# Longformer attention into a gated GeGLU block: the order of the work between the first and the second chunk

## Chip, cores and metric

The kernel runs on one core of one Trainium2 chip. The metric is device time in microseconds (us) of one execution; the time before is the median of three runs.

## What is computed

The reference, cut to what matters:

```python
# q, k, v: 8 batches x 8 heads x 576 positions x 64; 8 global positions
scores = q @ k.T / 8
mask = (abs(i - j) <= 32) | is_global[i] | is_global[j]
attn = softmax(where(mask, scores, -1e9))
x = (attn @ v) as 4608 tokens x 512
g, val = x @ w_gate, x @ w_val            # 512 -> 1536
ffn = (gelu(g) * val) @ w_out             # 1536 -> 512
out = x + sigmoid(x @ w_res) * ffn
```

## The kernel before, in words

A batch has nine windows of 64 positions. The 72 windows are cut into nine chunks of eight, so that a chunk is 512 tokens: chunk 0 is windows 0 to 7 of batch 0, chunk 1 the last window of batch 0 and seven of batch 1. The loop over chunks (L806) runs the feed-forward block of chunk c and, among it, the attention of chunk c + 1. The engines follow the order of the code (the schedule is written by hand); each engine has its own queue, in order.

For one chunk the steps are, by name:
- **Gate and value halves** (`ffn_steps`, L621): for each of twelve column blocks j, four matmuls of 512 columns give `g_ps` and four give `v_ps`; ScalarE takes the Gelu of `g_ps` into `gsb` (L635) and VectorE multiplies `gsb` with `v_ps` into `ht` (L638, "the product").
- **Turns** (`turn_pair`, L445, batches 0 and 1 only): TensorE transposes a pair of heads of k and q (p = 0 to 3, and -1 for the last 64 positions) into a bank of PSUM; VectorE copies k into `kt`, ScalarE copies q into `qt`.
- **Scores** (`scores`, L543): 16 small matmuls for each of four head groups give two banks `sc`; ScalarE takes the Exp (for chunk 1 in place, in PSUM), VectorE multiplies with the mask into `pt` (L556). A call has two banks, and a quad is half a chunk.
- **Global rows and columns**: `global_scores` (L467, tile `sg`), `global_exp` (L484: three Exps of ScalarE, then `gt` times `maskr` on VectorE, L494), `global_rows` (L496: matmuls into `sn`, then the multiplication into `vgs` on VectorE, L513).
- **Values** (`local_values`, L562, and `values`, L578) for each of four tiles t of 128 tokens: 16 matmuls of `pt` with V and two or four with `gt` and `vgs` into `nd`; VectorE takes the reciprocal and writes `xtok`. `split` (L559) says whether `nd` is one two-bank tile of the pool `psn` (tag "nd") or two single banks.
- **turn_x** (L602): `xtok` transposed into `xt`, the next chunk's input.
- **Residual gate** (`gate`, `open_gate`, L652 to L663): four matmuls into `r_ps`, Tanh on ScalarE.
- **Thirds** (`third`, L680): `f_ps` summed over twelve j in three groups of four matmuls; after the last, VectorE (L689) and GpSimd (L691) make the output, and SyncE stores it.

PSUM has three pools: `psm` with four banks (tag "mm": `g_ps`, `v_ps`, half of the scores, `r_ps`, `f_ps`), `pss` with two (tag "sc": turns, the other scores, `turn_x`), and `psn` with one tile of two banks (tag "nd": `sg`, `sn`, `nd`, one after the other). A tile waits until the one that held its place before it has been read.

For chunk 0 the order between its feed-forward block and chunk 1 is written out by hand (L814 to L934). Blocks j = 2 to 9 run one after the other, with `turn(0)` and `turn(1)` inside blocks 8 and 9. Blocks 10 and 11 run as gate, Gelu, `turn(2)`, gate, Gelu, `turn(3)`, then a dummy Exp that loads ScalarE's table, value, product, `turn(-1)`, value, product. Then L892 to L933: scores of quad 0, `global_scores`, residual gates 0 and 1 ahead of the scores of quad 1, `global_rows`, gate 2, `values(1, 0)`, gate 3, and the thirds with the other values among them.

Weights and the inputs of batch 1 are loaded as float32 into spare places by SyncE's queue and cast by GpSimd. `load_piece(n)` and `cast_piece(n)` move the weights: pieces 0 to 11 gate and value weights, 12 and 13 the residual weights `wr_t`, 14 to 19 the output weights `wo_t`. `load_raw` and `cast_pair` move k and q of a pair; `load_vraw(1)` and `cast_v(1, c)` the V of batch 1 in five parts, and `shift_on_chip(n)` copies V shifted by 64 rows into `vo`. SyncE's order before: pieces 10 and 11, raw pairs 0, 1, 2, 3, -1, pieces 12 and 13, V, pieces 14 to 19. GpSimd's order before (L852 to L868): pairs 0, 1, 2, 3, -1, pieces 12 and 13, V, `shift_on_chip(0)`, pieces 14 to 19, `shift_on_chip(3)`.

Of the kernel before, what the change touches and what calls it, by code (L numbers as in the profile page):

```python
# [9 lines left out]
BF16 = mybir.dt.bfloat16  # L10
# [13 lines left out]
def kernel(  # L24
# [116 lines left out]
    def load_piece(n):  # L141
        nc.sync.dma_start(staged(n), pieces[n][0])

    def cast_piece(n, copy):
        copy(pieces[n][1], staged(n))
# [411 lines left out]
        return mask  # L557

    def split(c, t):  # L559
        return c == 0 and t % 2 == 0 or c > 1 and t % 2 == 1  # L560

    def local_values(c, t):  # L562
        if split(c, t):
            pool, tag = (pss, "sc") if c else (psm, "mm")
            nds = [pool.tile([128, 512], F32, name=f"nd{hf}", tag=tag) for hf in range(2)]
            nd = None
        else:
            nd = psn.tile([128, 2, 512], F32, name="nd", tag="nd")
            nds = [nd[:, 0, :], nd[:, 1, :]]
        wins = [divmod(CH * c + 2 * t + e, NW) for e in range(2)]  # L570
        for h in range(H):
            for e, (b, i) in enumerate(wins):
                vw = ve[b % 2][:, i // 2, h, :] if i % 2 == 0 else vo[b % 2][:, i // 2, h, :]
                nc.tensor.matmul(nds[h // 4][64 * e:64 * e + 64, VG * (h % 4):VG * (h % 4) + VG],  # L574
                                 pt[:, h, 2 * t + e, :], vw, start=(h % 4 == 0), stop=False)
        return nd, nds, wins

    def values(c, t, begun=None):  # L578
# [10 lines left out]
        if split(c, t):  # L589
            for hf in range(2):  # L590
# [8 lines left out]
        nc.vector.tensor_tensor(xtok[c % 2][:, t, :].rearrange("p (a h d) -> p a h d", a=2, d=D),  # L599
                                num[:, :, :, 0:D], view(rden, 0, 128, 0, [[4, 2], [1, 4], [0, D]]), ALU.mult)  # L600

    def turn_x(c, t):  # L602
        mine = xt[c % 2][:, :, 128 * t:128 * t + 128]
        if c > 1:
            nc.sync.dma_start(mine, xtok[c % 2][:, t, :], transpose=True)
            return
        tx = pss.tile([128, NKT, 128], BF16, name="tx", tag="sc")
        for kk in range(NKT):
            nc.tensor.transpose(tx[:, kk, :], xtok[c % 2][:, t, 128 * kk:128 * kk + 128], ident)  # L609
        (nc.vector.tensor_copy if c or t == 3 else nc.scalar.copy)(mine, tx)  # L610
# [10 lines left out]
    def ffn_steps(c, j):  # L621
        x, held = xt[c % 2], {}

        def product(what, w):
            def emit(c0, c1):
                if what not in held:
                    held[what] = psm.tile([128, 512], F32, name=f"{what}_ps", tag="mm")
                for kk in range(NKT):
                    nc.tensor.matmul(held[what][:, c0:c1], w[:, kk, 128 * j:128 * j + 128], x[:, kk, c0:c1],  # L629
                                     start=(kk == 0), stop=(kk == NKT - 1))  # L630
            return emit

        def gelu():
            held["s"] = work.tile([128, 512], BF16, name="gsb", tag="gsb", bufs=3)
            nc.scalar.activation(held["s"], held["g"], ACTF.Gelu, bias=0.0, scale=1.0)  # L635

        def mul():
            nc.vector.scalar_tensor_tensor(ht[:, j, :], held["s"], 0.5, held["v"], ALU.mult, ALU.mult)  # L638

        def end():  # L640
            gelu()
            mul()

        return {"g": product("g", wg_t), "v": product("v", wv_t), "gelu": gelu, "mul": mul, "end": end}
# [118 lines left out]
    for n in range(4):  # L763
# [4 lines left out]
            load_raw(1, "kq"[n - 2], 0, nc.sync)  # L768
        if n == 1:
            fill(band, 1.0, [([[-1, 64]], 1, 0, ALU.is_ge, 0.0), ([[1, 64]], -1, 64, ALU.is_ge, 0.0)])  # L770
    for p in (1, 2, 3, -1):
        for what in "kq":
            load_raw(1, what, p, nc.sync)
    for n in range(4, 12):
        cast_piece(n, POOL)
    for n in (12, 13):
        load_piece(n)
    values(0, 0, begun_v[0])
# [22 lines left out]
    def turn(p):  # L801
        for what in "kq":
            turn_pair(1, p, what)

    turns = {8: lambda: turn(0), 9: lambda: turn(1)}
    for c in range(NCH):  # L806
        b = c + 1
        if b < B and c:
# [3 lines left out]
                gather(what, (c + 1) // 2 if c % 2 else c // 2 + 1)  # L812
        held = None
        for j in range(NFF):  # L814
            if c == 0 and j == 10:
                last = [ffn_steps(0, n) for n in (10, 11)]
                last[0]["g"](0, 512)
                last[0]["gelu"]()
                turn(2)
                last[1]["g"](0, 512)  # L820
                last[1]["gelu"]()
                turn(3)

                nc.scalar.activation(none, none, ACTF.Exp, bias=0.0, scale=1.0)
                last[0]["v"](0, 512)
                last[0]["mul"]()
                turn(-1)
                last[1]["v"](0, 512)
                last[1]["mul"]()
            elif c or 1 < j < 10:  # L830
                ffn_in(c, j, turns.get(j) if c == 0 else None)
            if c == 0:
                if j == 0:
                    mask_rows(0, NW)
                elif j == 1:
                    mask_rows(NW, NWM)
                    zero_k(1)
                elif j == 2:
                    zero_gt(1, nc.vector)
                    zero_globals(1)  # L840
                    for n in range(1, B // 2):
                        nc.vector.tensor_single_scalar(idx[:, n:n + 1], idx[:, 0:1], float(2 * H * S * n), ALU.add)
                elif j == 3:
                    zero_v(1, nc.vector)
                elif j == 4:
                    double_qk(0, 1)
                elif j == 6:
                    got = turn_globals(0, 1)
                    for what in "kq":
                        DVE(compact[what][:, 0:1, :], got[what])  # L850
                    spread_qk(1, compact, 0, {"k": DVE, "q": ACT})
                elif j == 5:  # L852
                    for p in (0, 1, 2, 3, -1):
                        for what in "kq":
                            cast_pair(1, p, what, POOL)
                    load_vraw(1)
                    for n in (14, 15):
                        load_piece(n)
                    for n in (12, 13):
                        cast_piece(n, POOL)  # L860
                    for n in range(16, 20):
                        load_piece(n)
                    for c5 in range(5):
                        cast_v(1, c5, POOL)
                    shift_on_chip(0, POOL)
                    for n in range(14, 20):
                        cast_piece(n, POOL)
                    shift_on_chip(3, POOL)  # L868
# [19 lines left out]
        if c == 0:  # L888
            def third(t, n):
                work_f[4 * t + 1 + n]()  # L890

            scores(1, 0, (0,))(0, 2)  # L892
            got = global_scores(1)
            scores(1, 0, (1,))(0, 2)
            global_exp(1, *got)
            for t in range(2):
                gates[t][0](now=False)
            first = scores(1, 1, (0,))
            gates[0][1]()
            second = scores(1, 1, (1,))  # L900
            gates[1][1]()
            global_rows(1)
            first(0, 2)
            gates[2][0]()
            values(1, 0)
            gates[3][0]()
            second(0, 2)
            for n in (1, 2):
                shift_on_chip(n, ACT)
            for what in "kq":  # L910
                load_second(what)
            cast_second("k", 0, NQT, ACT)
            values(1, 1)
            third(0, 0)
            third(1, 0)
            third(2, 0)
            turn_x(1, 0)
            third(3, 0)
            values(1, 2)
            turn_x(1, 1)  # L920
            third(0, 1)
            cast_second("q", 0, 1, POOL)
            values(1, 3)
            third(1, 1)
            turn_x(1, 2)
            third(2, 1)
            third(3, 1)
            turn_x(1, 3)
            for t in range(4):
                third(t, 2)  # L930
                if t == 1:
                    turn_qk(2, "k")
            cast_second("q", 1, NQT, POOL)  # L933
            continue  # L934
        jobs = {n: [] for n in range(16)}
        if c + 1 < NCH:
# [8 lines left out]
            jobs[1] += [lambda: half(0), gates[-1][1], lambda: held_mask[0](0, 4)]  # L945
            jobs[3].append(lambda: half(1))

            def two(t0):
                both = [local_values(c + 1, t) for t in (t0, t0 + 1)]
                for t in (t0, t0 + 1):  # L950
                    values(c + 1, t, both[t - t0])
                for t in (t0, t0 + 1):
                    turn_x(c + 1, t)

            jobs[4].append(lambda: two(0))
            jobs[8].append(lambda: two(2))
            jobs[5].append(lambda: held_mask[1](0, 2))
            jobs[6].append(lambda: held_mask[1](2, 4))
        for n in range(16):
# [35 lines left out]
```

## Time and profile before

| | |
|---|---|
| median of three runs | 387.99 us (387.68 to 388.45) |
| the profiled execution's own time | 387.56 us |
| its span in the trace | 385.9 us |
| TensorE busy | 372.7 us, 97% of the span |
| VectorE, ScalarE, GpSimd busy | 52%, 44%, 44% |
| chain that ended last | TensorE 94%, VectorE 3%, ScalarE 2% |

The profile is of one execution. A busy TensorE is the sum of its matmuls, each with its way through the array at the end; matmuls overlap, so the distance from one start to the next is shorter than the duration shown. The chain that ended last goes back from the last instruction, at each step to what released it. Where TensorE is nearly always busy, only its waits and its own work set the time.

### The profile page before, as it was taken

To read this page: it belongs to the slowest core of one execution; us is meant where nothing else is said; L and a number is where in the kernel's file an instruction comes from. 1 tells how busy PE (TensorE), PEld (TensorE's weight loads), DVE (VectorE), ACT (ScalarE), POOL (GpSimd) and SP (SyncE) were. 2 spreads that over 40 slices of the span, in tenths; PEclk is the share of its full clock that TensorE was granted. 3 is DMA by queue.
4 is the path that set the end of the run, shared out by engine and by line. 5 is a ranking of instruction groups with operands and counts; after the bars stand their busy time and mean duration, and the time that the engine had idled before them with its cause. 6 is when DMAs were issued, how large, how long until landed. Compare 5 with 4: busy or idle time off the path is not lost.

```text
span 385.9 us, 8474 instructions
## 1 busy us (share of the span) xinstructions
PE 372.7 (97%) x3332; PEld 187.7 (49%) x3332; DVE 200.8 (52%) x467; ACT 169.8 (44%) x285; POOL 168.2 (44%) x203
## 2 busy tenths in 40 slices
PE   3989989999999999999999999999999999999996
PEld 2664555444544454445444544454445544544444
DVE  7767774446734573367334744564445534553422
ACT  4753684436333643355334633372337233723321
POOL 7688684868355524661466138712501210121012
PEclk9999999999999999999999999999999999999999
DMA  8999999799949923999299939994990410041002
GB/s 242 239 373 366 249 321 220 172 178 162 136 97 152 195 58 109 127 199 103 82 146 175 114 97 135 182 102 117 110 158 4 109 57 0 3 109 56 0 29 82
DMA packets 156810, 53.70 MB, mean 139 GB/s; under 512 B 140194, under 2 KB 147234, under 8 KB 156770
## 3 DMA queue, kind: packets, MB, share of 16 engines
q1 hardware_dynamic: 80832, 42.80, 46.2%
q0 software_dynamic: 75392, 9.84, 43.7%
q8 instruction: 26, 0.43, 0.5%
q10 hardware_dynamic: 546, 0.52, 0.4%
q14 instruction: 14, 0.11, 0.1%
HBM read 39.19 MB, written 9.44 MB: 126 GB/s over the span
## 4 chain that ended last, share of the span: by engine, by line
PE 94%; DVE 3%; ACT 2%; issue 1%; POOL 0%; DVEq 0%; POOLq 0%; ACTq 0%
PE g_ps L629 24%; PE f_ps L685 24%; PE v_ps L629 24%; PE r_ps L655 8%; PE nd L574 3%; PE nd L586 3%; PE sc L533 3%; PE ss L480 1%; PE sg L471 1%; PE sn L509 1%; PE tk L450 1%; PE tq L450 1%; PE tx L609 0%; PE sc L522 0%; PE f_ps L671 0%
## 5 line engine op out<-in xcount | busy, mean ns | idle before, releaser
L638 DVE SCALAR_TENSOR_TENSOR ht<-gsb,v_ps 128x512 bf16<-128x512 bf16 x108 | 74.1, 687 | 95.8 <-PE v_ps L629 91.3
L635 ACT ACTIVATE gsb<-g_ps 128x512 bf16<-128x512 f32 x108 | 64.4, 597 | 121.1 <-PE g_ps L629 118.8
L691 POOL TENSOR_TENSOR ob<-prb,xtok 128x512 f32<-128x512 f32 x35 | 40.2, 1152 | 166.5 <-DVE prb L689 166.5
L629 PE MATMUL g_ps<-xt,wg_t 128*128 128x512 bf16 (+1 forms) x456 | 111.9, 368 | 0.0
L629 PE MATMUL v_ps<-xt,wv_t 128*128 128x512 bf16 (+1 forms) x456 | 111.9, 368 | 0.0
L685 PE MATMUL f_ps<-wo_t,ht 128*128 128x512 bf16 x420 | 98.0, 379 | 0.0
L629 PEld LDWEIGHTS <-wv_t 128*128 128x128 bf16 x456 | 43.5, 98 | 49.1
L629 PEld LDWEIGHTS <-wg_t 128*128 128x128 bf16 x456 | 43.4, 98 | 48.7
L685 PEld LDWEIGHTS <-ht 128*128 128x128 bf16 x420 | 39.8, 98 | 45.6
L663 ACT ACTIVATE rsb<-r_ps 128x512 bf16<-128x512 f32 x36 | 21.7, 606 | 68.0 <-PE r_ps L655 68.0
L689 DVE SCALAR_TENSOR_TENSOR prb<-rsb,f_ps 128x512 f32<-128x512 bf16 x35 | 24.1, 688 | 52.3 <-PE f_ps L685 50.7
L655 PE MATMUL r_ps<-wr_t,xt 128*128 128x512 bf16 x144 | 36.7, 378 | 1.0 <-ACT rsb L663 1.0
L540 ACT ACTIVATE pt<-sc 128x512 bf16<-128x512 f32 x64 | 33.2, 607 | 4.0 <-PE sc L533 3.2
L91 POOL DMA_DIRECT2D q_st<-in_q_dram x25 | 21.4, 861 | 18.8 <-DMA qt<-q_st 17.9
L99 POOL DMA_DIRECT2D ve<-in_v_dram x30 | 25.5, 865 | 0.0
L556 DVE TENSOR_TENSOR pt<-pt,maskw 128x512 bf16<-128x512 bf16 x56 | 21.8, 421 | 4.1 <-ACT pt L540 2.8
L91 POOL DMA_DIRECT2D k_st<-in_k_dram x25 | 21.1, 876 | 4.4 <-DMA kt<-k_st 3.2
L655 PEld LDWEIGHTS <-xt 128*128 128x128 bf16 x144 | 13.5, 97 | 13.2 <-issue 0.9
L574 PEld LDWEIGHTS <-pt 128*64 128x64 bf16 x576 | 11.1, 110 | 9.3 <-issue 4.6
L599 DVE TENSOR_TENSOR xtok<-nd,rden 128x512 bf16<-128x512 f32 x20 | 13.8, 691 | 0.8
L593 DVE TENSOR_TENSOR xtok<-nd,rden 128x256 bf16<-128x256 f32 x32 | 13.6, 425 | 1.1
L574 PE MATMUL nd<-ve,pt 128*64 128x65 bf16 x320 | 13.5, 196 | 0.7 <-DVE xtok L599 0.6
(174 smaller groups left out, 294.1 us busy)
## 6 DMA issues: line engine op xcount, KB each, us to landing
out_dram<-ob SPq DMA_DIRECT2D x35, 256.0 KB, 2.2
vo<-ve SPq DMA_DIRECT2D x12, 260.0 KB, 5.5
q_st<-in_q_dram POOLq DMA_DIRECT2D x20, 128.0 KB, 6.0
k_st<-in_k_dram POOLq DMA_DIRECT2D x20, 128.0 KB, 6.7
ve<-in_v_dram POOLq DMA_DIRECT2D x18, 128.0 KB, 6.4
wo_t<-in_k_dram SPq DMA_DIRECT2D x8, 256.0 KB, 5.6
vraw<-in_q_dram SPq DMA_DIRECT2D x8, 256.0 KB, 6.8
extra<-in_moe_w_out_dram SPq DMA_DIRECT2D x4, 512.0 KB, 7.5
```

Of the source, the lines that this page charges most:

```text
L91: nc.gpsimd.dma_start(dst[0:n, r, :].rearrange("p (h d) -> p h d", d=D), src[b].rearrange("h s d -> s h d")[128 * r:128 * r + n])
L99: nc.gpsimd.dma_start(t[p0:p1, c, :, 0:D], v[b].rearrange("h s d -> s h d")[s0 + p0:s0 + p1])
L540: nc.scalar.activation(sc if stay else mine, sc, ACTF.Exp, bias=0.0, scale=SCALE)
L556: nc.vector.tensor_tensor(m, x, view(maskw, 0, 128, 64 * i0, [[0, 2], [64, 4], [1, 64]]), ALU.mult)
L574: nc.tensor.matmul(nds[h // 4][64 * e:64 * e + 64, VG * (h % 4):VG * (h % 4) + VG], pt[:, h, 2 * t + e, :], vw, start=(h % 4 == 0), stop=F ...
L629: nc.tensor.matmul(held[what][:, c0:c1], w[:, kk, 128 * j:128 * j + 128], x[:, kk, c0:c1], start=(kk == 0), stop=(kk == NKT - 1))
L635: nc.scalar.activation(held["s"], held["g"], ACTF.Gelu, bias=0.0, scale=1.0)
L638: nc.vector.scalar_tensor_tensor(ht[:, j, :], held["s"], 0.5, held["v"], ALU.mult, ALU.mult)
L655: nc.tensor.matmul(r_ps, xt[c % 2][:, kk, 128 * t:128 * t + 128], wr_t[:, kk, :], start=(kk == 0), stop=(kk == NKT - 1))
L685: nc.tensor.matmul(held["f"], ht[:, j, 128 * t:128 * t + 128], wo_t[:, j, :], start=(j == 0), stop=(j == NFF - 1))
L689: nc.vector.scalar_tensor_tensor(prb, held["r"], 1.0, held["f"], ALU.add, ALU.mult)
L691: nc.gpsimd.tensor_tensor(ob, prb, xtok[c % 2][:, t, :], ALU.add)
```

## The change

It reorders work between chunk 0 and chunk 1. The gate halves of blocks 8 to 11 run first, each followed by its Gelu and one turn (pairs 0, 1, -1, 2); then the value half of block 8, `turn(3)` and the dummy Exp. The value halves and products of blocks 9, 10 and 11 go between the scores of chunk 1. `global_exp` goes ahead of the scores of quad 0's second half, and the masks of quad 1's first half ahead of `global_rows`. All four residual gates go behind the values of tiles 0 and 1, which run as a pair (`two`). Tiles 1 and 3 of chunk 1 use split banks: tile 1 from `psm`, tile 3 from `pss`. `gsb` has five buffers in place of three. The loads: pair -1 comes ahead of pairs 2 and 3, V of batch 1 ahead of pieces 12 and 13 on SyncE's queue; on GpSimd the casts of 12 and 13 come behind those of V and `shift_on_chip(0)`; the loads of 18 and 19 come behind the casts of 12 and 13 in the code.

```diff
     def split(c, t):
-        return c == 0 and t % 2 == 0 or c > 1 and t % 2 == 1
+        return t % 2 == (1 if c else 0)
...
-            pool, tag = (pss, "sc") if c else (psm, "mm")
+            pool, tag = (pss, "sc") if c > 1 or c == 1 and t > 1 else (psm, "mm")
...
+    def two(c, t0):
+        both = [local_values(c, t) for t in (t0, t0 + 1)]
+        for t in (t0, t0 + 1):
+            values(c, t, both[t - t0])
...
-            held["s"] = work.tile([128, 512], BF16, name="gsb", tag="gsb", bufs=3)
+            held["s"] = work.tile([128, 512], BF16, name="gsb", tag="gsb", bufs=5)
...
-    for p in (1, 2, 3, -1):
+    for p in (1, -1, 2, 3):
         for what in "kq":
             load_raw(1, what, p, nc.sync)
     for n in range(4, 12):
         cast_piece(n, POOL)
+    load_vraw(1)
     for n in (12, 13):
         load_piece(n)
...
-            if c == 0 and j == 10:
-                last = [ffn_steps(0, n) for n in (10, 11)]
-                last[0]["g"](0, 512)
-                last[0]["gelu"]()
-                turn(2)
-                last[1]["g"](0, 512)
-                last[1]["gelu"]()
+            if c == 0 and j == 8:
+                late = [ffn_steps(0, n) for n in range(8, NFF)]
+                for steps, p in zip(late, (0, 1, -1, 2)):
+                    steps["g"](0, 512)
+                    steps["gelu"]()
+                    turn(p)
+                late[0]["v"](0, 512)
+                late[0]["mul"]()
                 turn(3)
-
                 nc.scalar.activation(none, none, ACTF.Exp, bias=0.0, scale=1.0)
-                last[0]["v"](0, 512)
-                last[0]["mul"]()
-                turn(-1)
-                last[1]["v"](0, 512)
-                last[1]["mul"]()
-            elif c or 1 < j < 10:
-                ffn_in(c, j, turns.get(j) if c == 0 else None)
+            elif c or 1 < j < 8:
+                ffn_in(c, j)
...
-                    for p in (0, 1, 2, 3, -1):
+                    for p in (0, 1, -1, 2, 3):
                         for what in "kq":
                             cast_pair(1, p, what, POOL)
-                    load_vraw(1)
-                    for n in (14, 15):
-                        load_piece(n)
-                    for n in (12, 13):
-                        cast_piece(n, POOL)
-                    for n in range(16, 20):
+                    for n in range(14, 18):
                         load_piece(n)
                     for c5 in range(5):
                         cast_v(1, c5, POOL)
                     shift_on_chip(0, POOL)
+                    for n in (12, 13):
+                        cast_piece(n, POOL)
+                    for n in (18, 19):
+                        load_piece(n)
                     for n in range(14, 20):
                         cast_piece(n, POOL)
...
+            late_value(1)
             scores(1, 0, (0,))(0, 2)
+            late_value(2)
             got = global_scores(1)
+            global_exp(1, *got)
             scores(1, 0, (1,))(0, 2)
-            global_exp(1, *got)
-            for t in range(2):
-                gates[t][0](now=False)
+            late_value(3)
             first = scores(1, 1, (0,))
-            gates[0][1]()
             second = scores(1, 1, (1,))
-            gates[1][1]()
+            first(0, 2)
             global_rows(1)
-            first(0, 2)
-            gates[2][0]()
-            values(1, 0)
-            gates[3][0]()
             second(0, 2)
+            two(1, 0)
+            for n in range(4):
+                gates[n][0]()
             for n in (1, 2):
                 shift_on_chip(n, ACT)
             for what in "kq":
                 load_second(what)
             cast_second("k", 0, NQT, ACT)
-            values(1, 1)
             third(0, 0)
             third(1, 0)
+            turn_x(1, 0)
             third(2, 0)
-            turn_x(1, 0)
+            turn_x(1, 1)
             third(3, 0)
-            values(1, 2)
-            turn_x(1, 1)
+            two(1, 2)
             third(0, 1)
             cast_second("q", 0, 1, POOL)
-            values(1, 3)
             third(1, 1)
```

(`late_value(n)` is the value half of `late[n]` and its product. The later chunks' own `two` is renamed, with the same work.)

## Rows read from the trace of the kernel before

**Rows 1.** Windows: stretch, us, busy us by engine, granted clock, DMA, GB/s
```profile
52.00:58.00 6.00, 4.76 (x89) 2.73 (x82) 4.69 (x10) 5.00 (x10) 4.75 (x6) 1.00 1.02 368
...
70.40:110.30 39.90, 39.90 (x351) 19.30 (x350) 21.41 (x48) 17.12 (x28) 25.01 (x29) 1.00 1.16 153
```

**Rows 2.** PE timeline from block 8's gate: start, us, instruction [idle before]
```profile
38.15 1.03 PE L629 MATMUL g_ps<-xt,wg_t 128*128 128x512 bf16 x4
39.01 0.39 PE L450 MATMUL tk<-ident,k_st 128*128 128x128 bf16 x4
39.23 0.39 PE L450 MATMUL tq<-ident,q_st 128*128 128x128 bf16 x4
...
48.47 0.43 PE L471 MATMUL sg<-qt,kgz 128*32 128x288 bf16 x8
...
49.42 0.41 PE L533 MATMUL sc<-qt,kt 64*128 64x64 bf16 x16
49.76 1.90 PE L655 MATMUL r_ps<-wr_t,xt 128*128 128x512 bf16 x8
...
52.23 0.46 PE L509 MATMUL sn<-ve,ptg 128*16 128x130 bf16 x20
53.66 1.02 PE L655 MATMUL r_ps<-wr_t,xt 128*128 128x512 bf16 x4 [0.97 <-ACT rsb L663]
```

**Rows 3.** PE timeline, first value matmuls to chunk 1's first gate half
```profile
54.61 0.45 PE L574 MATMUL nd<-ve,pt 128*64 128x65 bf16 x16
54.99 0.62 PE L586 MATMUL nd<-vgs,gt 128*128 128x260 bf16 x4
55.45 1.02 PE L655 MATMUL r_ps<-wr_t,xt 128*128 128x512 bf16 x4
...
70.19 1.03 PE L629 MATMUL g_ps<-xt,wg_t 128*128 128x512 bf16 x4
```

**Rows 4.** ACT (ScalarE) timeline, from pair 3's q copy to the global Exps
```profile
45.36 0.58 ACT L457 COPY qt<-tq 128x512 bf16<-128x512 bf16 x1
45.96 1.28 ACT L824 ACT_TABLE_LOAD   x1
...
47.37 0.73 ACT L455 COPY qt<-tq 64x256 bf16<-64x256 bf16 x2
48.56 1.07 ACT L540 ACTIVATE sc<-sc 128x512 f32<-128x512 f32 x2 [0.47 <-PE sc L533]
...
50.95 0.50 ACT L490 ACTIVATE ptg<-sg 128x192 bf16<-128x192 f32 x2
51.34 0.66 ACT L493 ACTIVATE gt<-sg 128x576 bf16<-128x576 f32 x1
```

**Rows 5.** DVE (VectorE) timeline, from block 10's product to vgs
```profile
46.25 0.69 DVE L638 SCALAR_TENSOR_TENSOR ht<-gsb,v_ps 128x512 bf16<-128x512 bf16 x1 [0.47 <-PE v_ps L629]
46.85 0.85 DVE L455 COPY kt<-tk 64x256 bf16<-64x256 bf16 x2
...
49.17 2.58 DVE L556 TENSOR_TENSOR pt<-sc,maskw 128x512 bf16<-128x512 f32 x4 [0.75 <-ACT sc L540]
52.03 0.57 DVE L494 TENSOR_TENSOR gt<-gt,maskr 128x576 bf16<-128x576 bf16 x1 [0.27 <-ACT gt L493]
52.74 0.70 DVE L513 TENSOR_TENSOR vgs<-sn,head 128x520 bf16<-128x520 f32 x1
```

**Rows 6.** POOL (GpSimd) timeline: last raw pair, residual piece 13, V's last part
```profile
43.59 0.61 POOL L267 CAST q_st<-vraw 128x512 bf16<-128x512 f32 x1
...
46.81 1.04 POOL L145 CAST wr_t<-extra 128x1024 bf16<-128x1024 f32 x1 [0.76 <-DMA extra<-in_moe_w_res_dram]
...
51.68 0.61 POOL L190 CAST ve<-wo_t 96x512 bf16<-96x512 f32 x1 [0.43 <-DMA wo_t<-in_v_dram]
```

**Rows 7.** PE timeline near the start of the execution
```profile
6.63 0.61 PE L450 MATMUL tk<-ident,k_st 128*128 128x128 bf16 x4 [0.86 <-DVE k_st L270]
...
11.41 0.63 PE L450 MATMUL tq<-ident,q_st 128*128 128x128 bf16 x4
```

More of the change, by code (lines that the diff above doesn't have):

```diff
@@ L803, in turn @@
             turn_pair(1, p, what)
-    turns = {8: lambda: turn(0), 9: lambda: turn(1)}
     for c in range(NCH):
@@ L890, in third, with late_value @@
                 work_f[4 * t + 1 + n]()
+            def late_value(n):
+                late[n]["v"](0, 512)
+                late[n]["mul"]()
+            late_value(1)
             scores(1, 0, (0,))(0, 2)
+            late_value(2)
             got = global_scores(1)
+            global_exp(1, *got)
             scores(1, 0, (1,))(0, 2)
-            global_exp(1, *got)
-            for t in range(2):
-                gates[t][0](now=False)
+            late_value(3)
             first = scores(1, 1, (0,))
-            gates[0][1]()
             second = scores(1, 1, (1,))
-            gates[1][1]()
+            first(0, 2)
             global_rows(1)
-            first(0, 2)
-            gates[2][0]()
-            values(1, 0)
-            gates[3][0]()
             second(0, 2)
+            two(1, 0)
+            for n in range(4):
+                gates[n][0]()
             for n in (1, 2):
@@ L946, with pair @@
             jobs[3].append(lambda: half(1))
[L948 to L951, printed above, removed]
+            def pair(t0):
+                two(c + 1, t0)
                 for t in (t0, t0 + 1):
                     turn_x(c + 1, t)
-            jobs[4].append(lambda: two(0))
-            jobs[8].append(lambda: two(2))
+            jobs[4].append(lambda: pair(0))
+            jobs[8].append(lambda: pair(2))
             jobs[5].append(lambda: held_mask[1](0, 2))
```

## Prediction

> **What bounds the kernel now.** I read the busy time by window first. In chunk 1's feed-forward block and the stage after it TensorE is busy for 39.90 of 39.90 us; in the stage that the change reorders it is busy for 4.76 of 6.00 us [rows 1]. So no later stage can give anything, and a delay in this stage passes to the end undiminished: the whole question is when TensorE starts chunk 1's first gate half, now 70.19 [rows 3]. Then the timelines of the engines. On TensorE's, one wait stands out: the third residual gate starts at 53.66 after 0.97 us, held by a Tanh that frees its bank [rows 2]. On ScalarE's, the table load of the dummy Exp, 1.28 us from 45.96, lies ahead of the first Exp at 48.56 [rows 4]. On VectorE's, the four masks take 2.58 us from 49.17 and the multiplication into `vgs` starts at 52.74 [rows 5]. In this stage no engine is full; they wait for each other in the order in which the code queues them.
>
> Up to block 7 nothing moves, so both kernels start block 8's gate half at 38.15 [rows 2]. I follow the new order from there on each queue.
>
> **Gate halves and turns first.** The half takes 0.86 from start to start, a pair of turns 2 x 0.22 (39.01 to 39.23) [rows 2]. Four halves and four turns: 38.15 + 4 x (0.86 + 0.45) = 43.39. Block 8's value half ends at 44.25, `turn(3)` starts its q at 44.47. ScalarE's copy of it starts some 0.47 later, 44.95. The table load followed that copy's start by 0.60 and the next work came 1.41 after the load's start [rows 4], so ScalarE is ready for the first Exp at 46.96. Before, the first Exp started at 48.56: 1.6 us are won here. The scores themselves are ready sooner: block 9's value half ends at 45.57, their banks are free when VectorE has copied pair 3's k (product 0.60 to the next start [rows 5], copy about 0.7, done near 45.8), and the call takes 0.34 (49.42 to 49.76) [rows 2].
>
> The raw pairs are only reordered. The last cast of them started at 43.59 and took 0.61 [rows 6]; pair 3 takes that place, and its q is needed at 44.47. Pair -1, half as large, is needed at 41.6 and comes third, before its need. This costs nothing, by some 0.3 us; if that cover goes, the cost is what it is late. More `gsb` buffers cost nothing: four Gelus now stand ahead of their products, which five buffers hold and three would not.
>
> **The chain on VectorE.** From here it has one piece of work behind another: two masks, block 10's product, `gt` times `maskr`, two masks, block 11's product, two masks, and only then `vgs`. The first mask follows its Exp's start by 0.61 (48.56 to 49.17) [rows 4, 5]: 47.57. A mask costs 2.58/4 = 0.64, a product 0.60, `gt` times `maskr` at most 0.57 (I take 0.53, since it overlaps its follower), `vgs` 0.70 [rows 5]. Sum: 6 x 0.64 + 2 x 0.60 + 0.53 + 0.70 = 6.27, ending at 53.84. ScalarE keeps ahead: its global Exps start near 48.25, when `sg` is done (0.95 from 48.47 to 49.42 [rows 2], behind block 10's value half), and take 0.39 + 0.66 [rows 4], so that `gt` is ready at 49.3 and VectorE gets to it at 49.45.
>
> TensorE meanwhile issues scores, block 10's value half, `sg`, scores, block 11's value half, scores, `sn`. Without waits it would have `sn` behind it at about 50.4. The last scores wait for a "mm" bank: the fourth allocation before it is a score bank whose mask ends near 50.7, so `sn` (about 0.5 [rows 2]) is done near 51.6. Then it meets the wait that the change adds: `nd` of tile 0 needs the place of `sn`, so it waits until `vgs` has been written, 53.84 + 0.06 = **53.9**. Everything is queued behind it: `nd` of tile 1, whose banks are free, both tiles' other matmuls, and all four residual gates, which need nothing of VectorE. Before, two gates had run ahead of this point and `nd` started at 54.61 [rows 3]. So the added idle time is some 1.1 + 2.3 us, in place of the 0.97 and some shorter waits.
>
> **From `nd` to the next block.** Work that remains: 4 x 0.38 of local values (54.61 to 54.99), 0.46 for tile 0's four matmuls and 3 x 0.23 for the others' two, 4 gates x 0.86 [rows 3], 12 thirds x 0.86 of the same shape as a gate, 4 x 0.22 of `turn_x`: 1.52 + 1.15 + 3.44 + 10.32 + 0.88 = 17.3. I count no wait in it: tile 1's split costs VectorE two more instructions, hidden behind the gates; tiles 2 and 3 start near 62.7, while ScalarE, behind the last Tanh near 59.5, has copied V's shifted parts 1 and 2 by 62.1 (four of about 0.64). That slack is thin, 0.6 us; it would be what is late next. 53.9 + 17.3 = 71.2, against 70.19: **+1.0 us**.
>
> **The loads.** V's five DMAs pass pieces 12 and 13 on SyncE, and the V casts and the two copies of `shift_on_chip(0)` pass their casts on GpSimd. V is needed by `sn` from about 51.0. Before, its last cast ran from 51.68 to 52.29 [rows 6], so the move takes a wait away that the new order would have had; but `vgs` starts at 53.1 anyway because of VectorE, so even V at its old time costs nothing. The bytes before piece 14 are the same, so the output weights keep their time, and pieces 18 and 19 wait on SyncE for the casts of 12 and 13 without emptying the DMA queue. The residual weights come later: their second cast started at 46.81 [rows 6] and will end between 47.85, as now, and 56.5 (V's last cast at its old end 52.29, two copies of 0.7, two casts of 1.04 with 0.76 of waiting [rows 6]). The gates need them from 55.3, half of them from 55.75. The cost is thus between nothing and 0.8 us; I take nothing, since the same bytes flow and V's place is taken by 12 and 13 near 52.
>
> **Sum.** The profiled execution took 387.56 us, so 388.6 in its terms. It is 0.43 below the median of the runs, 387.99, to which I add the same 1.0: **389.0 us**, slower by 0.26%. About 0.2%, 0.8 us, is what a measurement of this kernel can tell from no change, so this is close to the border: `nd` at 53.7 divides them.
>
> **Rivals.**
> - *The chain starts earlier.* If ScalarE were ready when the first scores are (45.9 + 0.42), VectorE would start 0.6 us earlier: +0.4, 388.4, within 0.2%. The table load, which follows pair 3's copy in the code, speaks against it; mask and product steps a few hundredths shorter would add to the same side. Chance 0.31, with those cases of my own sum that stay under 0.8 us.
> - *VectorE is not the bound at `nd`*, on the faster side. If `vgs` came right behind `sn`, `nd` would wait for 0.7 of multiplication after about 50.6 and start near 51.4: 387.99 + 1.0 - 2.5 = 386.5. It decides from `nd` below 52.1, that is, 1.8 us less work ahead of `vgs` than I count. VectorE's queue in the order of the code speaks against it; the 1.6 us won at the first Exp, for it. Chance 0.14.
> - *The residual weights are late*: GpSimd, not VectorE, holds the first gates, +0.8 on top, 389.8. Byte counts speak against it, SyncE's slow issue of V for it. Chance 0.09.
> - *The clock falls in the hole.* TensorE would have some 3.4 us of waiting in 4 us ahead of 53.9. Near the start of the execution its transposes took 0.61 to 0.63 for four, from 6.63 to 11.41 [rows 7], against 0.39 later [rows 2]: the lower level, 1.2 GHz, by their own durations, over 4.8 us; the granted clock of the stage itself reads 1.00, 2.4 GHz [rows 1], and the gate after 0.97 us of waiting ran with the usual 1.02 [rows 2, 3]. As long at half speed would cost half of it, 2.4: 391.4. Chance 0.06, as the wait grows from one to two and a half.
> - *The change doesn't do what it says*: V arrives no earlier. As shown, no cost; it is in the forecast.
>
> The Trainium skill's "TensorE: Matmul & The Clock Gate" (HAM oscillation) says that TensorE's clock is halved after a long enough idle stretch and comes back only after sustained work. By that rule the time would be 391.4 where the gate acts on this wait, and 389.0 where it doesn't; no row before shows a wait of this length in mid-kernel, so the trace leaves it open.
>
> **Chances and range.** My forecast proper has 0.40, spread from 388.8 to 389.5. Slower by over 0.2%: 0.40 + 0.09 + 0.06 = 0.55; within 0.2%: 0.31; faster: 0.14. The range reaches from 386.9, into the faster case, to 390.3, above late residual weights; it leaves out the clock case and the lower half of the faster one, 0.13.
>
> **What would show it.** Right: the first Exp near 47.0; VectorE without a gap from 47.6 to 53.8, with `vgs` last; TensorE's longest wait at L574, over 2 us, released by `vgs`; chunk 1's first gate half near 71.2; L663 no longer ahead of TensorE's waits. Wrong: `nd` before 53, a wait at the gates released by GpSimd's cast, a wait of tiles 2 and 3 for `vo`, or matmuls after the wait with twice their duration.

## The result and the profile after

The changed kernel takes 390.33 us (median of six runs, 389.55 to 390.8), the kernel before 388.09 beside it: ratio 1.0056, 95% interval 1.0042 to 1.0069. It is slower by 2.24 us, the side that was forecast, by more than twice the amount of the likeliest case: 0.03 us above the range as it was given, and just inside it, at 390.23, when the 2.24 are added to the 387.99 that the forecast started from. The profiled execution took 390.4 us with a span of 388.7.

TensorE's timeline of the changed kernel, with the same columns as [rows 2, 3]:

```profile
38.90 1.03 PE L634 MATMUL g_ps<-xt,wg_t 128*128 128x512 bf16 x4
...
46.52 0.58 PE L533 MATMUL sc<-qt,kt 64*128 64x64 bf16 x16
...
50.27 0.43 PE L533 MATMUL sc<-qt,kt 64*128 64x64 bf16 x17
51.38 0.39 PE L533 MATMUL sc<-qt,kt 64*128 64x64 bf16 x15 [0.67 <-DVE pt L556]
...
51.77 0.46 PE L509 MATMUL sn<-ve,ptg 128*16 128x130 bf16 x20
54.37 0.51 PE L574 MATMUL nd<-ve,pt 128*64 128x65 bf16 x16 [2.15 <-DVE vgs L513]
...
55.25 1.48 PE L586 MATMUL nd<-vgs,gt 128*128 128x260 bf16 x6
56.52 4.36 PE L660 MATMUL r_ps<-wr_t,xt 128*128 128x512 bf16 x16
...
73.17 1.03 PE L634 MATMUL g_ps<-xt,wg_t 128*128 128x512 bf16 x4
```

Chunk 1's first gate half starts at 73.17 in place of 70.19 [rows 3]. 2.98 us later is more than the runs differ by, and the first 0.75 of it is not the change's: block 8's gate half starts at 38.90 in place of 38.15 [rows 2], though nothing ahead of it on TensorE was touched. The timelines of the first microseconds show where most of that came from, the kernel before and then the changed one:

```profile
12.28 0.64 PE L522 MATMUL sc<-xt,ident_big 128*128 128x512 bf16 x2
...
13.20 0.40 PE L450 MATMUL tk<-ident,k_st 128*128 128x128 bf16 x4
```

```profile
12.28 1.04 PE L522 MATMUL sc<-xt,ident_big 128*128 128x512 bf16 x2
...
13.76 0.40 PE L450 MATMUL tk<-ident,k_st 128*128 128x128 bf16 x4
```

The same two matmuls of 512 columns took 0.64 in one execution and 1.04 in the other: the clock's first rise fell some half a microsecond later there, which is 0.56 by the transposes behind. The other 0.19 came ahead of chunk 0's first `nd`, which waited 0.90 for its `vgs` in place of 0.53. Such shifts belong to the execution: the last transpose of `tg` ahead of the stage lies at 37.12 here, and between 36.13 and 37.50 in the profiles of experiments 1, 2, 4 and 5, which are the same kernel up to there. What follows is therefore read from a common point, that transpose of `tg` (36.37 before, 37.12 after): to the first value matmuls it was 18.24 us and is 17.25, from there to chunk 1's first gate half 15.58 and is 18.80. Together +2.23, which is what the medians differ by.

So the way to `nd` got 1.0 us shorter, where the prediction had 0.7 (54.61 to 53.9), and what remains behind it got longer by 3.22. The remaining work has three more residual gates in it (one stood behind `nd` in [rows 3], now all four do), but the first rows behind the wait also run slowly: six matmuls of `vgs` take 1.48 and sixteen of the gates 4.36, where experiments 1 to 3 below have 0.84 and 3.6. Busy time by window of the changed kernel, columns as in [rows 1] (the eighth group is the granted clock, ahead of the DMA share and GB/s):

```profile
50.00:52.00 2.00, 1.33 (x57) 0.89 (x56) 2.00 (x5) 2.00 (x6) 0.43 (x1) 1.00 1.04 388
52.00:53.00 1.00, 0.22 (x16) 0.14 (x5) 1.00 (x2) 1.00 (x3) 0.75 (x2) 1.00 1.03 389
53.00:54.00 1.00, 0.00 (x0) 0.00 (x0) 1.00 (x3) 0.04 (x1) 0.89 (x1) 1.00 1.06 393
54.00:55.00 1.00, 0.63 (x29) 0.63 (x30) 1.00 (x3) 0.00 (x0) 0.79 (x1) 0.81 1.05 389
55.00:56.00 1.00, 1.00 (x15) 0.73 (x12) 0.51 (x1) 0.00 (x0) 0.69 (x2) 0.50 1.04 385
...
57.00:58.00 1.00, 1.00 (x4) 0.41 (x3) 0.93 (x5) 0.00 (x0) 0.96 (x1) 0.50 1.13 358
58.00:59.00 1.00, 1.00 (x7) 0.39 (x4) 0.42 (x1) 0.60 (x1) 0.73 (x1) 0.99 1.11 249
```

TensorE is busy for 1.33 of 2 us, 0.22 of 1 and not at all, and then the granted clock is 0.81, 0.50 and 0.50: the lower level, 1.2 GHz, from 54.6 to 58.0. The mean granted clock of the execution shows it too, 0.996, and all six runs have 0.995 or 0.996; the kernel before has 1.00 or 0.998 to 0.999 in all but one of the 52 runs made beside the experiments.

ScalarE and VectorE in the same execution, columns as before:

```profile
45.77 0.58 ACT L457 COPY qt<-tq 128x512 bf16<-128x512 bf16 x1 [0.72 <-PE tq L450]
46.37 1.28 ACT L829 ACT_TABLE_LOAD   x1
...
47.77 1.06 ACT L540 ACTIVATE sc<-sc 128x512 f32<-128x512 f32 x2
...
49.45 0.66 ACT L493 ACTIVATE gt<-sg 128x576 bf16<-128x576 f32 x1
```

```profile
48.38 1.29 DVE L556 TENSOR_TENSOR pt<-sc,maskw 128x512 bf16<-128x512 f32 x2 [1.00 <-ACT sc L540]
49.59 0.68 DVE L643 SCALAR_TENSOR_TENSOR ht<-gsb,v_ps 128x512 bf16<-128x512 bf16 x1
50.19 0.45 DVE L494 TENSOR_TENSOR gt<-gt,maskr 128x576 bf16<-128x576 bf16 x1
50.63 1.29 DVE L556 TENSOR_TENSOR pt<-sc,maskw 128x512 bf16<-128x512 f32 x2
51.84 0.68 DVE L643 SCALAR_TENSOR_TENSOR ht<-gsb,v_ps 128x512 bf16<-128x512 bf16 x1
52.43 1.28 DVE L556 TENSOR_TENSOR pt<-sc,maskw 128x512 bf16<-128x512 f32 x2
53.63 0.69 DVE L513 TENSOR_TENSOR vgs<-sn,head 128x520 bf16<-128x520 f32 x1
```

The first Exp starts at 47.77, 47.0 without the 0.75, against 48.56 [rows 4]; from 48.38 on VectorE goes from one piece of the predicted chain to the next, `gt` at 50.19 between them, and `vgs` ends at 54.32, just ahead of `nd` at 54.37. GpSimd's timeline has V's last cast at 47.96 in place of 51.68 and the second residual piece at 52.85 in place of 46.81 [rows 6]:

```profile
47.96 0.61 POOL L190 CAST ve<-wo_t 96x512 bf16<-96x512 f32 x1 [0.73 <-DMA wo_t<-in_v_dram]
...
52.85 1.04 POOL L145 CAST wr_t<-extra 128x1024 bf16<-128x1024 f32 x1 [0.25 <-DMA extra<-in_moe_w_res_dram]
```

### The profile page after: what moved, and what is told of

Read it like the earlier page. It is cut to its first block, busy times and chain, and to the rows that moved or that the text cites. A ratio compares the mean times of both kernels' runs of the same rounds, so it can differ in the third digit from the quotient of the medians.

```text
span 388.7 us, 8481 instructions
## 1 busy us (share of the span) xinstructions
PE 374.1 (96%) x3332; PEld 188.4 (48%) x3332; DVE 202.3 (52%) x471; ACT 169.7 (44%) x285; POOL 168.2 (43%) x203
## 4 chain that ended last, share of the span: by engine, by line
PE 93%; DVE 5%; issue 1%; ACT 1%; POOL 0%; DVEq 0%; POOLq 0%; ACTq 0%
PE g_ps L634 24%; PE f_ps L690 24%; PE v_ps L634 23%; PE r_ps L660 8%; PE nd L586 3%; PE nd L574 3%; PE sc L533 2%; DVE pt L556 1%; PE ss L480 1%; PE tk L450 1%; PE tq L450 1%; PE sg L471 1%; PE sc L522 0%; PE sn L509 0%; DVE gt L494 0%
## 5 line engine op out<-in xcount | busy, mean ns | idle before, releaser
L660 PEld LDWEIGHTS <-xt 128*128 128x128 bf16 x144 | 13.8, 99 | 13.2 <-issue 1.0
L593 DVE TENSOR_TENSOR xtok<-nd,rden 128x256 bf16<-128x256 f32 x36 | 15.3, 424 | 1.2
L533 PEld LDWEIGHTS <-kt 64*128 64x128 bf16 x576 | 10.0, 96 | 8.4 <-issue 6.7
```

Of the source, the lines that this page charges most:

```text
L660: nc.tensor.matmul(r_ps, xt[c % 2][:, kk, 128 * t:128 * t + 128], wr_t[:, kk, :], start=(kk == 0), stop=(kk == NKT - 1))
```

## Experiments

Each run is compared with runs of the kernel before on the same chip (388.08 us in the first four experiments, 388.07 in the last two). All are edits of the changed kernel. Stage length means from the last `tg` to chunk 1's first gate half: 33.82 before, 36.05 in the changed kernel.

**1. `vgs` ahead of the first masks of quad 1.**

```diff
-            first(0, 2)
             global_rows(1)
+            first(0, 2)
             second(0, 2)
```

> The changed kernel with global_rows ahead of the masks of quad 1's first half, so that vgs has two masks less ahead of it on VectorE. Theory (VectorE's queue holds the first value matmuls, and the clock falls because that wait is 2.15 us long): vgs starts 1.25 us earlier, the wait shrinks to about 0.9, the clock stays at 1.00, and the first residual gate then waits about 0.4 for the mask that frees its bank; 0.85 + 1.4 us less than the changed kernel, 388.1. Rival (the clock falls because the whole stretch is sparse, whatever its longest wait): the granted clock still shows 0.5 and the time is 389.5. Rival (vgs is not what holds nd): no change, 390.3.

Measured: 388.37 us, ratio to the kernel before 1.0004 (0.9988 to 1.002), stage 34.37, mean clock 0.999 to 1.00 in eleven of twelve runs and 0.996 in one. TensorE's timeline of this kernel:

```profile
52.36 0.39 PE L533 MATMUL sc<-qt,kt 64*128 64x64 bf16 x15 [1.27 <-DVE pt L556]
...
54.16 0.45 PE L574 MATMUL nd<-ve,pt 128*64 128x65 bf16 x16 [0.96 <-DVE vgs L513]
...
55.96 3.63 PE L660 MATMUL r_ps<-wr_t,xt 128*128 128x512 bf16 x16 [0.31 <-DVE pt L556]
```

Moving one line gives back 2.0 of the 2.24 us. The wait at `nd` is 0.96 and the gates wait 0.31 for a mask, both near what was expected, and the sixteen gate matmuls take 3.63. So VectorE's queue held `nd`. But `nd` comes 0.59 us sooner after `tg` than in the changed kernel, and not 1.25: the wait of the scores ahead of it has grown to 1.27, since `gt` times `maskr` took 1.14 in this execution, while GpSimd was casting beside it (more on that in experiment 4):

```profile
50.56 1.14 DVE L494 TENSOR_TENSOR gt<-gt,maskr 128x576 bf16<-128x576 bf16 x1
```

```profile
50.35 1.03 POOL L145 CAST wr_t<-extra 128x1024 bf16<-128x1024 f32 x1
```

Most of the 2.0 us is thus the clock's, which stayed up in eleven of twelve runs. That the shorter wait at `nd` kept it up is not shown: the longest wait in this profile is 1.27, and in experiment 5 the clock fell behind shorter ones.

**2. The same wait, with TensorE kept busy in it.** Block 11's value half is computed twice more and not used.

```diff
             global_rows(1)
+            for _ in range(2):
+                late[3]["v"](0, 512)
             second(0, 2)
```

> The changed kernel with block 11's value half computed twice more into its own bank, behind sn, in the wait for vgs: 1.73 us of matmuls whose results nobody needs, and no other edit. Theory: nd starts as late as in the changed kernel, but the granted clock stays at 1.00 and the sixteen gate matmuls take 3.6 us in place of 4.36; 1.4 us less, 388.9. Rival (the matmuls behind the wait are slow for another reason, such as the DMA traffic): no change, 390.3.

Measured: 389.28 us, 1.0027 (1.0015 to 1.004), stage 34.82, mean clock 0.999 or 1.00 in all twelve runs.

```profile
52.76 1.89 PE L634 MATMUL v_ps<-xt,wv_t 128*128 128x512 bf16 x8 [0.35 <-DVE ht L643]
54.58 0.45 PE L574 MATMUL nd<-ve,pt 128*64 128x65 bf16 x16
...
55.90 3.62 PE L660 MATMUL r_ps<-wr_t,xt 128*128 128x512 bf16 x16
```

`nd` comes no earlier, and the gates take 3.62: more work on TensorE made the kernel 1.05 us faster. So it was the idle TensorE that let the clock fall, and the two parts come apart: with the clock up, the order alone costs 1.2 us against the kernel before in this run, and the clock the rest. It gave 0.4 less than expected: in the profiled execution `nd` starts 0.35 later after `tg` than in the changed kernel, and `gt` times `maskr`, ahead of it on VectorE, takes 0.87 in place of 0.45.

**3. V behind the residual weights again**, on SyncE's queue and on GpSimd.

```diff
-    load_vraw(1)
     for n in (12, 13):
         load_piece(n)
+    load_vraw(1)
...
+                    for n in (12, 13):
+                        cast_piece(n, POOL)
                     for c5 in range(5):
                         cast_v(1, c5, POOL)
                     shift_on_chip(0, POOL)
-                    for n in (12, 13):
-                        cast_piece(n, POOL)
```

> The changed kernel with V of batch 1 loaded and cast behind the residual weights again, as before the change. Theory (V's place is worth nothing, as vgs waits for VectorE anyway): V's last cast ends near 52.5 in place of 48.6, sn waits for it by under 1 us, vgs starts as in the changed kernel; 390.3, within 0.4. Rival (V's place matters): vgs and nd start 0.5 to 1 us later and the time is 391.

Measured: 390.66 us, 1.006 (1.0036 to 1.0084). The same, as the theory had it: in the profiled execution four matmuls of `sn` wait 0.22 for V, and `nd` starts 17.25 us after `tg`, exactly as in the changed kernel.

```profile
52.47 0.23 PE L509 MATMUL sn<-ve,ptg 128*16 128x130 bf16 x4 [0.22 <-POOL ve L190]
54.46 0.45 PE L574 MATMUL nd<-ve,pt 128*64 128x65 bf16 x16 [1.76 <-DVE vgs L513]
...
55.78 3.61 PE L660 MATMUL r_ps<-wr_t,xt 128*128 128x512 bf16 x16
```

This run told more than it was made for. In the profiled execution and one other of its six the clock did not fall (388.95 and 389.26 us, mean clock 1.00), in three it did (390.62 to 391.0, 0.996), and one at 0.991 took 391.88. One kernel at either level: some 1.6 us. And its stage at full clock, 34.47, prices the order alone in a trace: +0.65. The times of these two executions lie 0.9 and 1.2 above the median of the kernel before, so the order alone costs between 0.65 and 1.2.

**4. The chain ahead of `vgs` made short.**

```diff
-            late_value(3)
+            late[3]["v"](0, 512)
+            global_rows(1)
+            late[3]["mul"]()
             first = scores(1, 1, (0,))
             second = scores(1, 1, (1,))
-            first(0, 2)
-            global_rows(1)
             second(0, 2)
+            first(0, 2)
             two(1, 0)
```

> The changed kernel with sn ahead of the scores of quad 1, vgs right behind quad 0's masks on VectorE, block 11's product next, and the masks of quad 1's second half (whose banks the gates need) ahead of those of its first. Theory: nd starts 1.75 us earlier, the gates don't wait for banks, the clock stays at 1.00: 1.75 + 1.4 less than the changed kernel, 387.2, faster than before by 0.9. Rival (the clock falls all the same): 388.6. Rival (residual weights hold the gates, whose second cast ends near 53.9): 387.2 plus what they wait.

Measured: 387.62 us, 0.9985 (0.9971 to 0.9999), 0.5 us less than the kernel before where 0.9 was expected. `nd` starts 15.84 us after `tg`, 1.4 sooner than in the changed kernel, against 1.75 expected. VectorE's timeline shows where the rest went, and GpSimd's beside it:

```profile
49.20 0.91 DVE L494 TENSOR_TENSOR gt<-gt,maskr 128x576 bf16<-128x576 bf16 x1
```

```profile
49.19 0.61 POOL L190 CAST ve<-wo_t 96x512 bf16<-96x512 f32 x1 [1.50 <-DMA wo_t<-in_v_dram]
49.87 0.72 POOL L107 COPY vo<-ve 64x520 bf16<-64x520 bf16 x1
```

`gt` times `maskr` took 0.91, while GpSimd cast V. In the changed kernel GpSimd had nothing to do from 49.91 to 51.57, and it took 0.45. Two of twelve runs, the profiled one among them, have a mean clock of 0.996, though the longest wait in the stage is 0.81 us. Its windows:

```profile
51.00:52.00 1.00, 0.19 (x14) 0.17 (x7) 1.00 (x3) 1.00 (x4) 0.94 (x2) 1.00 1.05 397
52.00:53.00 1.00, 0.98 (x34) 0.81 (x34) 1.00 (x2) 0.51 (x2) 1.00 (x2) 0.99 1.06 397
53.00:54.00 1.00, 1.00 (x7) 0.68 (x6) 1.00 (x3) 0.00 (x0) 0.93 (x2) 0.50 1.04 385
```

A wait of 0.8 does not keep the clock safe, then; the kernel before, with 0.97 [rows 2], had one such run in 52.

**5. Two gates put into the wait**, loads as in the change.

```diff
             global_rows(1)
+            for n in range(2):
+                gates[n][0]()
             second(0, 2)
             two(1, 0)
-            for n in range(4):
+            for n in range(2, 4):
                 gates[n][0]()
```

> The changed kernel with the first two residual gates back ahead of the first value matmuls, behind sn, in the wait for vgs; loads as in the change. Theory (the wait costs because nothing that was ready stands in it, and the gates put there in turn wait for the residual weights, whose cast the change has moved to 53.9): the second half of gate 0 starts near 53.95, nd near 55.3 in place of 54.4 in the changed kernel's own times, the clock stays up, and the end is 0.8 + 1.6 us sooner than in the changed kernel: 388.0, about as before. Rival (residual weights in time): nd as in the changed kernel, 387.1. Rival (the clock falls all the same): 389.5.

Measured: 389.02 us, 1.003 (1.0008 to 1.0053). Five runs with the clock up took 387.54 to 388.03, where the theory has 388.0; seven with a mean of 0.996 or less took 388.96 to 392.46. TensorE's waits in the profiled execution, one with the clock down, show what the gates met (us waited in all, number of waits, the longest):

```profile
PE r_ps L660 <- POOL wr_t L145: 1.4, 2, 0.8
```

The residual weights, behind V since the change, came too late for gates at this place, so the wait was cut in two and not filled. With the clock up this order costs nothing against the kernel before; in the seven other runs the clock took more than that back.

**6. The wait filled with work that is ready.** Residual weights ahead of V as in experiment 3, and:

```diff
             late_value(3)
+            for n in range(2):
+                gates[n][0]()
             first = scores(1, 1, (0,))
             second = scores(1, 1, (1,))
-            first(0, 2)
             global_rows(1)
+            gates[2][0]()
             second(0, 2)
+            first(0, 2)
             two(1, 0)
-            for n in range(4):
-                gates[n][0]()
+            gates[3][0]()
```

> The changed kernel with the residual weights ahead of V again (SyncE's loads and GpSimd's casts), gates 0 and 1 behind block 11's value half, gate 2 behind sn, gate 3 behind the values of tiles 0 and 1; vgs on VectorE ahead of all masks of quad 1, the masks of its second half first. Theory: TensorE's wait for vgs is filled with useful work, nd starts near 53.7 (in the times of the kernel before) with three gates behind it, chunk 1's first gate half near 68.8 in place of 70.2: 386.7, faster than before by 1.4, and the clock stays at 1.00. Rival (the output weights, whose second cast ended at 56.4 before, hold the first thirds): 387.2. Rival (V, cast to 52.3, holds sn and the gain is lost): 388.

Measured: 386.63 us, 0.9967 (0.9957 to 0.9977), stage 32.40, mean clock 0.998 to 1.00 in all twelve runs.

```profile
49.78 2.07 PE L660 MATMUL r_ps<-wr_t,xt 128*128 128x512 bf16 x8
...
52.81 1.04 PE L660 MATMUL r_ps<-wr_t,xt 128*128 128x512 bf16 x3
53.78 0.45 PE L574 MATMUL nd<-ve,pt 128*64 128x65 bf16 x16
...
54.73 0.19 PE L574 MATMUL nd<-vo,pt 128*64 128x65 bf16 x1 [0.37 <-DVE pt L556]
...
68.97 1.03 PE L634 MATMUL g_ps<-xt,wg_t 128*128 128x512 bf16 x4
```

Three gates run ahead of `nd`, which starts right behind the third; one wait of 0.37 for a mask is left. This is 1.4 us faster than the kernel before and 3.7 faster than the change, most of whose parts it keeps: gate halves and turns first, the value halves between the scores, the split of tile 1.

## Why the prediction was right or wrong

- **The bound and the side**: right that a delay in this stage passes on whole: +2.23 in the stage, +2.24 in the medians. The side is in part luck. The order alone costs 0.65 us (trace of experiment 3) to 1.2 (experiment 2); the prediction's own border to "no change" is 0.8. What took the time well past it is the fall of the clock, which the forecast proper didn't have.
- **Gate halves first**: right. The first Exp starts at 47.0 in the times of before, as worked out. The reordered raw pairs cost next to nothing: block 11's gate half ran 0.12 longer, start to start, ahead of `turn(2)` than its 0.86.
- **The chain on VectorE**: right in its members and their order, a little too long. A mask cost 0.60 from start to start (1.21 from 48.38 to 49.59 for two) and not 2.58/4 = 0.64, which had the end of the last one in it; `gt` took 0.45 for 0.53. So `nd` came 0.28 sooner than forecast. Experiment 1 shows that it was `vgs` that held it. The prediction misread one row on the way: before, three gates and not two had run ahead of `nd`, two from 49.76 and one at 53.66 [rows 2]; its sum doesn't use that.
- **From `nd` on**: 17.3 forecast, 17.22 in experiments 2 and 3 with the clock up. At full clock the order costs +0.65 in a trace (experiment 3), for +1.0 forecast; the difference, 0.35, is the chain's length for the most part.
- **The step that failed is the clock.** It stood as a rival, "the clock falls in the hole", at a chance of 0.06 and a price of 2.4 on top. It fell in six of six runs and cost 18.80 - 17.22 = 1.58. The forecast had the waits that caused it, some 3.4 us in 4, and took the 0.97 us of the kernel before as a sign that the clock bears such things. The measured waits were 0.67 and 2.15, and with matmuls put into the longer one the clock stayed up in twelve of twelve runs (experiment 2). The price was mis-sized too: half of the time at the lower level was the right rule, but that time is 3.4 us here, 54.6 to 58.0, and not the 4.8 of the start; half of 3.4 is 1.7.
- **The time lies at the upper end of the range by luck.** That end stood for late residual weights, which held nothing here. The forecast's +1.0, less the 0.35 by which the order itself came cheaper, plus 1.58 for the clock makes the 2.23.
- By the rule of the Trainium skill's "TensorE: Matmul & The Clock Gate" (What's actually happening) the clock is halved after idling and comes back with sustained work. The trace agrees in kind: 0.50 behind the wait, 1.00 from 58.0 on under dense matmuls. The waits did not have to be one idle stretch: short matmuls stood between them.
- **The loads**: right that V's place is worth nothing here (experiment 3). Left out was what it costs a better order: residual weights at 53.9 keep gates from filling the wait (experiment 5).
- **"The chain starts earlier", "VectorE is not the bound", "residual weights are late"**: the first Exp came when forecast, but the shorter steps on VectorE that the first rival also names did come; `nd` at 53.6 in the times of before rules out the second, which needed it below 52.1; of the third, no gate of the changed kernel waited for the weights, as 53.89 lies ahead of 56.52.
- Open: none of the six runs of the changed kernel had the clock up, so what its order costs at full clock is read from experiments 2 and 3. Not tried: the same stage with the table load moved, and the turns without the change's other parts.

## What to carry to other kernels

When work is moved behind a wait, ask what is left to stand in it: the change moved the work that had been ready there (residual gates) out of the one place where TensorE has to wait for VectorE's queue, and a longer wait cost its own length and then the clock behind it. Order the slower engine's queue by who waits for what: one line, `vgs` ahead of two masks that nobody needed yet, was worth 2.0 us, most of it through the clock. And price a wait near the top of TensorE's dense stretch with the clock's part in it, from a run at either level.

## What the runs showed of the hardware that was not expected

- Whether the clock falls is not the same in all runs of one kernel: it did in 6 of 6 runs of the changed kernel, 4 of 6 with V behind, 7 of 12 of experiment 5, 2 of 12 of experiment 4, 1 of 12 of experiment 1, 1 of 52 of the kernel before, and in none of experiments 2 and 6. The waits of the profiled executions don't order these: in experiment 5 the longest is 0.98 (a bank of scores) and the three above 0.3 make 2.38, in experiment 1 they are 1.27 and 2.54. What decides it stays open.
- The multiplication `gt` times `maskr`, the one step of the chain with both inputs in SBUF, took 0.45 where GpSimd idled beside it (changed kernel, experiments 3 and 6) and 0.84 to 1.14 where GpSimd was casting (experiments 1, 2, 4 and 5); it then ended 0.31 to 0.32 us after GpSimd's instruction did, and so did the 0.57 of the kernel before, behind V's last cast [rows 5, 6]. The masks, whose scores lie in PSUM, kept to about 0.60 from start to start in all of them. The Trainium skill's "SBUF — State Buffer" (Who interferes with whom) has a rule for it: an instruction of VectorE with two inputs in SBUF and one of GpSimd that reads SBUF exclude each other for a whole instruction. The eight traces agree.
- Matmuls that nobody needed, 1.73 us of them, made the kernel 1.05 us faster (experiment 2).
- The granted clock reads 1.00 in the first 12 us of the kernel before, though the matmuls there take the time of the lower level [rows 7]; the moment at which they speed up, 12.3 there and past 13.8 in experiments 1 to 3, differs between executions and moves what follows by half a microsecond and more.
